# The end of an attention stage on one Trainium2 core: exponentials read straight from the banks, values by key tile, row sums spread by a product

## The chip, the cores and the metric

The kernel runs on one core of one Trainium2 chip. A core has five engines that run side by side and meet through semaphores: TensorE (PE in the profile, its weight loads PEld), VectorE (DVE), ScalarE (ACT), GpSimd (POOL) and SyncE (SP), which issues most DMAs. Matrix products go to eight banks of accumulator memory, from which DVE and ACT read. Everything else lies in the on-chip buffer (128 partitions) or in DRAM. A small q behind an engine's name (SPq, DVEq) means its sequencer, which loads registers, branches, waits and issues DMAs.

The metric is device time in microseconds of one execution; lower is better. Of several runs the median is taken.

## What is computed

From the reference: `x` is 2048 tokens of 448 features; 16 heads of 28 features share one key and one value projection; a token-mixing MLP runs beside the attention, and a sigmoid gate mixes the two.

```python
def _A_ref(x, wq, wk, wv, wo):
    B, S, D = x.shape
    H = 16
    Dh = D // H
    q = (lambda x, *d: x.transpose(*d))((x @ wq).reshape(B, S, H, Dh), 0, 2, 1, 3)
    k = x @ wk
    v = x @ wv
    scores = jnp.einsum("bhqd,bkd->bhqk", q, k) * (Dh ** -0.5)
    p = _softmax(scores, axis=-1)
    o = jnp.einsum("bhqk,bkd->bhqd", p, v)
    return (lambda x, *d: x.transpose(*d))(o, 0, 2, 1, 3).reshape(B, S, H * Dh) @ wo
...
x = A_x
g = _sigmoid((x * gate_w).sum(-1, keepdims=True))
a = _A_ref(x, A_wq, A_wk, A_wv, A_wo)
b = _B_ref(x, B_w1, B_w2, B_w3, B_w4)
return g * a + (1 - g) * b
```

## The kernel before

The MLP and the projections fill the first 410 us or so and are not touched. Attention is the last stage. It works through 16 units `u`: four blocks of 512 queries, and in each four groups of four heads. A unit has eight stretches `v` of two key tiles (128 keys each). All engines' instructions stand in the order in which the code writes them (`manual_schedule`); nothing is reordered later. The eight banks stand in a list: `take()` takes the first, whoever has read it last puts it back at the end (`banks.append`), and `bank(name)` does both at once.

A stretch (loop at line 886) does, in PE's order: scores of its two key tiles (`scores`, line 826, four heads in four banks for each), two half output products of an earlier unit (`wo_half`, line 807), and the value products of the stretch before (`values`, line 863). `exps` (line 845) turns the four score banks of a key tile into exponentials in the order `READ` = 0, 3, 1, 2. For heads 0, 1, 2, ACT does so straight from the bank (line 855). For head 3 (`DRAIN`), DVE copies the bank to the buffer (line 852), and at the end of the stretch `late_exps` (line 858) exponentiates the two copies in one pass of 1024 columns.

`values` multiplies, for each half of the 512 queries, both key tiles of all four heads with `vext`, whose first column is ones. Row 32j of the sum `o` therefore holds the sum of head j's exponentials; the 28 rows behind it hold the unnormalised output. Inside a unit DVE adds the banks into `o` (line 876). For all units but the last, the sums leave by a DMA that lays them out 128 x 16 (`sums_begin`, line 765), are checked against a limit and inverted (`recip`, line 770), go through DRAM and come back spread over 32 rows each (line 778); `norm` (line 781) multiplies. `wo_job` (line 787) multiplies 128 tokens with the output weights and adds the result, times the gate, to `ot`; in the last group of a block `ot` is sent out.

The last unit has no later work to hide behind. From line 915 on, its values are computed without adding, four additions of 128 queries follow (line 963), and PE transposes `o` by token tiles (line 968), so that the sums stand along the tokens: DVE then inverts 8 numbers per partition for two tiles (line 931) and multiplies (line 935); PE transposes back (line 940), ACT copies (line 941), and four `wo_job`s follow with `end` (line 946) as the last step: DVE adds for token tiles 0, 2, 3, ACT and POOL for tile 1, and SP (ACT for tile 1) issues the output's DMA. `keep_warm` puts small products into PE's waits.

The check of all sums ends in one number: `worst` per partition (line 982), transposed (line 989), reduced and turned to an integer flag (lines 992, 993). Every engine loads the flag (line 996) and branches over a slower fallback for the whole attention (line 999), which these inputs do not need. Behind it SP waits for all DMAs, and the engines meet at a barrier (line 1071 in the trace).

Of the kernel before, what the change touches and what calls it, by code (L numbers as in the profile page):

```python
# [9 lines left out]
F32 = mybir.dt.float32  # L10
F32R = mybir.dt.float32r
AF = mybir.ActivationFunctionType
ALU = mybir.AluOpType
# [29 lines left out]
def gated_mix_kernel(  # L43
# [686 lines left out]
    with tc.tile_pool(name="s3", bufs=1, reuse_waits="tile") as s3, \  # L730
# [7 lines left out]
        def take():  # L738
            return banks.pop(0)
# [15 lines left out]

        on_of = {}

        good = s3.tile([P, 8, 4], F32, name="good")
        nc.gpsimd.memset(good, 1.0)

        def check(sums, c):
            g = good[:, c:c + sums.shape[1]]
            nc.vector.scalar_tensor_tensor(g, sums, LIMIT, g, op0=ALU.is_le, op1=ALU.min)

        def sums_begin(u, o):
            rt = s3.tile([P, 16], F32, tag="rt", bufs=2, name=f"rt_{u}")
# [2 lines left out]

        def recip(u, o, rt, checked=True):  # L770
            if checked:
                check(rt.rearrange("p (a b) -> p a b", b=4), 0)
            rr = s3.tile([P, 16], F32, tag="rr", bufs=2, name=f"rr_{u}")
            nc.vector.reciprocal(rr, rt)
            rd = dram.tile([4, 512], F32, tag="rd", bufs=2, name=f"rd_{u}")
            nc.sync.dma_start(rd.rearrange("j (a b) -> (j a) b", b=16), rr)
# [7 lines left out]

        ot_of = {}

        def wo_job(u, t, end=None, cols=slice(0, D)):
            b, g = divmod(u, NG)
            n = 4 * b + t
            ps = take()  # L790
            for j in range(4):
                tok = slice(t * P + 32 * j, t * P + 32 * j + 32)
                nc.tensor.matmul(ps[32 * j:32 * j + 32, cols], on_of[u][:, tok], wof[:, g, cols],  # L793
                                 start=True, stop=True, tile_position=(0, 32 * j))
# [3 lines left out]
            if end:  # L798
                end(t, n, ps[:, 0:D], before)
            else:  # L800
                nc.vector.scalar_tensor_tensor(ot_of[n][:, cols], ps[:, cols], gg[:, n:n + 1], before,
                                               op0=ALU.mult, op1=ALU.add)
                if g == NG - 1 and cols.stop == D:
                    nc.sync.dma_start(out[0, n * P:(n + 1) * P, :], ot_of[n])
            banks.append(ps)

        def wo_half(u, i):
            t, h = divmod(i, 2)
            wo_job(u, t, None, slice(224 * h, 224 * h + 224))

        weigh_x1(NT - 4, NT)

# [29 lines left out]
            free.append(t)  # L842
            return t

        def exps(u, kt, bs):
            ps = p_of[u, kt] = {}
            for j in READ:
                if j == DRAIN:
                    if kt % 2 == 0:
                        pd_of[u, kt // 2] = turn_of(pd_free)  # L850
                    ps[j] = pd_of[u, kt // 2][:, kt % 2, :]
                    nc.vector.tensor_copy(ps[j], bs[j])  # L852
                else:
                    ps[j] = turn_of(p_free)
                    behind[kt % 2] = nc.scalar.activation(ps[j], bs[j], AF.Exp, scale=SCALE)  # L855
                banks.append(bs[j])

        def late_exps(u, v):
            pd = pd_of.pop((u, v))
            ins = nc.scalar.activation(pd, pd, AF.Exp, scale=SCALE)  # L860
            tc.add_manual_dep(ins.ins, behind[0].ins.name, SYNC, reason="one wait of ACT for its own writes per stretch")

        def values(u, v, add=True):
            if v == 0:
                o_of[u] = s3.tile([P, 512], F32, tag="o", bufs=2, name=f"o_{u}")
            pvs = []
            for q in (slice(0, 256), slice(256, 512)):
                pv = take()
                for kt in (2 * v, 2 * v + 1):
                    for j in range(4):  # L870
                        nc.tensor.matmul(pv[32 * j:32 * j + 32, q], vext[:, kt, :], p_of[u, kt][j][:, q],  # L871
                                         start=(kt % 2 == 0), stop=(kt % 2 == 1), tile_position=(0, 32 * j))
                if v == 0:
                    nc.vector.tensor_copy(o_of[u][:, q], pv[:, q])
                elif add:
                    nc.vector.tensor_add(o_of[u][:, q], o_of[u][:, q], pv[:, q])  # L876
                pvs.append(pv)
                if add:
                    banks.append(pv)
            return pvs  # L880

        READ = (0, 3, 1, 2)
        DRAIN = 3
        WO_AT = (4, 5, 6, 7)

        for k in range(NU * NV):
# [26 lines left out]
        assert not sums and not norms  # L913

        u = NU - 1
        pvs = values(u, NV - 1, False)
        o = o_of[u]
        on_of[u] = s3.tile([P, 512], F32, tag="on", bufs=2, name=f"on_{u}")
        toks = [slice(t * P, (t + 1) * P) for t in range(4)]
        tp = [bank(f"ot_{i}").rearrange("p (t n) -> p t n", t=4) for i in range(2)]  # L920
        tq = [bank(f"oq_{t}") for t in range(4)]
        spare = tq[3]
        tq = [ps[:, 0:P] for ps in tq]
        rr = s3.tile([P, 2, 2, 4], F32, name="rr4")
        on4 = s3.tile([P, 4, P], F32, name="on4")

        def sums_of(i):
            return tp[i][:, 0:2, 0:128:32]

        def tail_sums(i):  # L930
            nc.vector.reciprocal(rr[:, i], sums_of(i))

        def tail_on(t):
            i, k = divmod(t, 2)
            nc.vector.tensor_tensor(on4[:, t].rearrange("p (j d) -> p j d", j=4),
                                    tp[i][:, k].rearrange("p (j d) -> p j d", j=4),
                                    rr[:, i, k].unsqueeze(2).broadcast_to([P, 4, 32]), ALU.mult)

        def tail_back(t):
            nc.tensor.transpose(tq[t], on4[:, t], ident)  # L940
            nc.scalar.copy(on_of[u][:, toks[t]], tq[t])

        y = s3.tile([P, D], F32, name="y")
        outs = []

        def end(t, n, ps, before):
            if t == 1:
                nc.scalar.activation(y, ps, AF.Copy, scale=gg[:, n:n + 1])
                nc.gpsimd.tensor_tensor(ot_of[n], y, before, ALU.add)
            else:  # L950
                nc.vector.scalar_tensor_tensor(ot_of[n], ps, gg[:, n:n + 1], before, op0=ALU.mult, op1=ALU.add)
            queue = nc.scalar if t == 1 else nc.sync
            queue.dma_start(out[0, n * P:(n + 1) * P, :], ot_of[n])

        def tail_wo(t):
            wo_job(u, t, end)

        def keep_warm(n):
            for _ in range(n):
                nc.tensor.matmul(spare[:, 0:256], warm[:, 0:P], warm, start=True, stop=True)  # L960

        for t in range(4):
            nc.vector.tensor_add(o[:, toks[t]], o[:, toks[t]], pvs[t // 2][:, toks[t]])
        with tc.block():
            tc.mark_branch_hint_location("redo", "LikelyTaken", [mybir.EngineType.PE])
            keep_warm(5)
            for t in range(4):
                nc.tensor.transpose(tp[t // 2][:, t % 2], o[:, toks[t]], ident)
        keep_warm(3)
        tail_sums(0)  # L970
        tail_on(0)
        tail_on(1)
        tail_back(0)
        tail_back(1)
        keep_warm(2)
        tail_sums(1)
        tail_on(2)
        tail_on(3)
        for i in range(2):
            check(sums_of(i), 4 + 2 * i)  # L980
        worst = s3.tile([P, 1], F32, name="worst")
        nc.vector.tensor_reduce(worst, good, axis=AX.XY, op=ALU.min)
        tail_back(2)
        keep_warm(2)
        tail_wo(0)
        tail_back(3)
        tail_wo(1)
        tw = bank("worst_t")[0:1, 0:P]
        nc.tensor.transpose(tw, worst, ident)
        least = s3.tile([1, 1], F32, name="least")  # L990
        redo = s3.tile([1, 1], mybir.dt.int32, name="redo")
        nc.vector.tensor_reduce(least, tw, axis=AX.X, op=ALU.min)
        nc.vector.tensor_scalar(redo, least, -1.0, 1.0, op0=ALU.mult, op1=ALU.add)
        tail_wo(2)
        tail_wo(3)
        again = nc.values_load(redo, min_val=0, max_val=1)


# [76 lines left out]
```

## Time and profile before

| | us |
|---|---|
| median of 3 runs | 927.33 |
| lowest, highest | 925.99, 928.0 |
| the profiled execution | 926.66 |
| its span, from first to last instruction | 924.7 |
| granted TensorE clock in it, mean | 0.999 |

All durations are from the one profiled execution, whose span is 2.0 us shorter than its time. Times are counted from the start of the span. In a row of the timeline stand start, length, engine, line, operation, output<-inputs, shape and count; in brackets the engine's idle time before it and what ended it. A count over one merges neighbours; a float matrix product is recorded as two passes, so four heads make eight records.

The attention stage has 128 stretches. Between 910 and 914 us, in the last unit's own end, the engines were busy as follows (us of each):

| us from the start | PE | DVE | ACT | POOL |
|---|---|---|---|---|
| 910 to 912 | 2.00 | 1.07 | 0.00 | 0.00 |
| 912 to 914 | 1.85 | 1.53 | 0.72 | 0.00 |

### The profile page before, as it was taken

How to read it: one execution, taken by the hardware profiler on the slowest of the kernel's cores; microseconds unless marked ns; L12 is line 12 of the kernel's file. 1: busy time of each engine (PE TensorE's matmuls, PEld its weight loads, DVE VectorE, ACT ScalarE, POOL GpSimd, SP SyncE). 2: the span in 40 equal slices, each digit the busy share in tenths (PEclk: the TensorE clock that was granted, in tenths of full speed). 3: DMA queues.
4: the chain of work that ended last, by engine and by line, in shares of the span. 5: the costliest groups of instructions: out<-in, count | busy, mean ns of one | idle time of the engine just before them, and what ended most of it. 6: DMA issues, size and time to landing. Idle time of an engine off the chain costs nothing.

```text
span 924.7 us, 23960 instructions
## 1 busy us (share of the span) xinstructions
PE 911.7 (99%) x10051; PEld 647.5 (70%) x10051; DVE 542.2 (59%) x1081; ACT 634.5 (69%) x1134; POOL 104.2 (11%) x135
## 2 busy tenths in 40 slices
PE   9999999999999999999999999999999999999996
PEld 6788888888888888875566666666655656666663
DVE  4665263631435736446666666666666666666664
ACT  5542434432231232259999999999999999999993
POOL 2233200212000440031000000000000000000000
PEclk9999999999999999999999999999999999999999
DMA  9801534130122042110000001001011100110001
GB/s 303 300 27 26 169 128 129 22 84 21 33 65 60 19 104 61 38 54 23 25 23 6 26 14 53 26 26 26 8 41 46 26 4 24 35 45 3 14 14 44
DMA packets 40691, 50.72 MB, mean 55 GB/s; under 512 B 8752, under 2 KB 26880, under 8 KB 40576
## 3 DMA queue, kind: packets, MB, share of 16 engines
q1 hardware_dynamic: 37552, 43.65, 16.4%
q10 hardware_dynamic: 3024, 5.47, 1.6%
q8 instruction: 80, 1.31, 0.6%
q14 instruction: 35, 0.29, 0.1%
HBM read 37.04 MB, written 11.93 MB: 53 GB/s over the span
## 4 chain that ended last, share of the span: by engine, by line
PE 93%; ACT 3%; DMA 2%; DVE 1%; issue 0%; SPq 0%; DVEq 0%; ACTq 0%
PE bank L871 23%; PE bank L831 21%; PE bank L793 7%; PE acc L655 5%; PE acc L654 5%; PE acc L656 5%; PE g L132 4%; PE g L131 4%; PE g L133 4%; ACT p L855 2%; DMA xkv<-in_xT_dram 2%; PE hs L437 1%; PE hs L436 1%; PE hs L438 1%; PE g L135 1%; PE g L134 1%
## 5 line engine op out<-in xcount | busy, mean ns | idle before, releaser
L855 ACT ACTIVATE p<-bank 128x512 f32<-128x512 f32 x768 | 391.0, 626 | 5.8 <-PE bank L831 5.8
L871 PE MATMUL bank<-p,vext 128*32 128x256 f32 x3072 | 243.9, 379 | 2.1 <-ACT p L855 2.1
L871 PE MATMUL bank<-pd,vext 128*32 128x256 f32 x1024 | 242.2, 379 | 0.3 <-ACT pd L860 0.3
L852 DVE COPY pd<-bank 128x512 f32<-128x512 f32 x256 | 176.6, 691 | 53.2 <-PE bank L831 52.3
L871 PEld LDWEIGHTS bank<-p,vext 128*32 128x32 f32 x3072 | 125.1, 110 | 85.8 <-ACT p L855 5.1
L644 ACT ACTIVATE gh<-g 128x512 fp32r<-128x512 f32 x55 | 32.8, 597 | 189.5 <-PE g L135 189.5
L876 DVE TENSOR_TENSOR o<-o,bank 128x256 f32<-128x256 f32 x222 | 93.5, 421 | 91.3 <-ACT p L855 51.0
L860 ACT ACTIVATE pd<-pd 128x1024 f32<-128x1024 f32 x128 | 143.0, 1117 | 0.0
L831 PE MATMUL bank<-qh,kH 30*128 30x512 f32 x1024 | 119.6, 443 | 0.0
L871 PEld LDWEIGHTS bank<-pd,vext 128*32 128x32 f32 x1024 | 111.6, 110 | 1.3 <-ACT pd L860 0.7
L646 DVE TENSOR_TENSOR gl<-gf,gh 128x512 fp32r<-128x512 f32 x55 | 37.9, 690 | 125.5 <-ACT gf L645 125.4
L831 PE MATMUL bank<-qh,kL 28*128 28x512 f32 x1024 | 106.2, 394 | 0.0
L831 PE MATMUL bank<-ql,kH 28*128 28x512 f32 x1024 | 105.7, 389 | 0.0
L831 PEld LDWEIGHTS bank<-qh,kH 30*128 30x128 f32 x1024 | 60.9, 182 | 58.4 <-ACT p L855 47.0
L655 PE MATMUL acc<-w4l,gh 128*128 128x448 f32 x220 | 80.4, 366 | 0.0
L654 PE MATMUL acc<-w4h,gh 128*128 128x448 f32 x220 | 80.3, 365 | 0.0
L656 PE MATMUL acc<-w4h,gl 128*128 128x448 f32 x220 | 80.1, 364 | 0.0
L793 PE MATMUL bank<-wof,on 128*32 128x224 f32 (+1 forms) x992 | 73.1, 370 | 0.3 <-ACT p L855 0.3
L132 PE MATMUL g<-al,w3h 128*128 128x512 f32 x168 | 65.8, 392 | 0.0
L131 PE MATMUL g<-ah,w3h 128*128 128x512 f32 x168 | 65.6, 390 | 0.0
L133 PE MATMUL g<-ah,w3l 128*128 128x512 f32 x168 | 65.5, 390 | 0.0
L831 PEld LDWEIGHTS bank<-ql,kH 28*128 28x128 f32 x1024 | 52.6, 185 | 8.3
(196 smaller groups left out, 1164.8 us busy)
## 6 DMA issues: line engine op xcount, KB each, us to landing
qd<-qf ACTq DMA_DIRECT2D x16, 256.0 KB
qm<-qd SPq DMA_DIRECT2D x16, 256.0 KB
qr<-qd SPq DMA_DIRECT2D x16, 256.0 KB
rb<-rd SPq DMA_DIRECT2D x15, 256.0 KB
x<-in_x_dram SPq DMA_DIRECT2D x4, 896.0 KB
xd<-xt SPq DMA_DIRECT2D x16, 224.0 KB
w34raw<-in_w_dram SPq DMA_DIRECT2D x7, 512.0 KB
out_dram<-ot SPq DMA_DIRECT2D x15, 224.0 KB
```

Of the source, the lines that this page charges most:

```text
L131: nc.tensor.matmul(ps, wh[:, c, :], ah[:, c, :], start=(c == 0), stop=False)
L132: nc.tensor.matmul(ps, wh[:, c, :], al[:, c, :], start=False, stop=False)
L133: nc.tensor.matmul(ps, wl[:, c, :], ah[:, c, :], start=False, stop=False)
L654: nc.tensor.matmul(ps, gh[:, tok], w4h[i][:, k, :], start=(f == 0), stop=False)
L655: nc.tensor.matmul(ps, gh[:, tok], w4l[i][:, k, :], start=False, stop=False)
L656: nc.tensor.matmul(ps, gl[:, tok], w4h[i][:, k, :], start=False, stop=(f == stop))
L793: nc.tensor.matmul(ps[32 * j:32 * j + 32, cols], on_of[u][:, tok], wof[:, g, cols], start=True, stop=True, tile_position=(0, 32 * j))
L831: nc.tensor.matmul(bs[j], w, a, start=(i == 0), stop=(i == 2), tile_position=(32 * j, 0))
L852: nc.vector.tensor_copy(ps[j], bs[j])
L855: behind[kt % 2] = nc.scalar.activation(ps[j], bs[j], AF.Exp, scale=SCALE)
L860: ins = nc.scalar.activation(pd, pd, AF.Exp, scale=SCALE)
L871: nc.tensor.matmul(pv[32 * j:32 * j + 32, q], vext[:, kt, :], p_of[u, kt][j][:, q], start=(kt % 2 == 0), stop=(kt % 2 == 1), tile_position ...
```

## The change

It rewrites the end of the last unit. In the very last stretch no bank is drained by DVE: all eight exponentials are read by ACT from the banks, and there is no late pass. Its value products go by key tile, first both halves of tile 14, then both of tile 15, and two additions of 256 queries follow. The sums are no longer brought to the tokens by transposing: a matrix `spread` of ones in four 32 x 32 patterns (row 32j to columns 32j to 32j+31) is multiplied with `o`, so that each row of a bank holds its head's sum. DVE inverts that bank over all 512 queries (in pieces of 128, 128, 256) and multiplies. The check of the last unit's sums takes the DMA path that the other units use. Tiles 0, 1, 2 are finished by `wo_job` with DVE's addition, tile 3 in two halves of 224 columns; SP and ACT issue the outputs in turn. The flag is computed after all of that. Of twelve warming products two are left.

```diff
-        good = s3.tile([P, 8, 4], F32, name="good")
+        good = s3.tile([P, 4, 4], F32, name="good")
         nc.gpsimd.memset(good, 1.0)
+        spread = s3.tile([P, P], F32, name="spread")
+        nc.gpsimd.memset(spread, 0.0)
+        for j in range(4):
+            nc.gpsimd.memset(spread[32 * j:32 * j + 1, 32 * j:32 * j + 32], 1.0)
...
-        def wo_job(u, t, end=None, cols=slice(0, D)):
+        def wo_job(u, t, cols=slice(0, D), send=None):
...
+            nc.vector.scalar_tensor_tensor(ot_of[n][:, cols], ps[:, cols], gg[:, n:n + 1], before,
+                                           op0=ALU.mult, op1=ALU.add)
+            if send:
+                send(n, cols)
+            elif g == NG - 1 and cols.stop == D:
+                nc.sync.dma_start(out[0, n * P:(n + 1) * P, :], ot_of[n])
...
-        def exps(u, kt, bs):
+        def exps(u, kt, bs, drain=True):
             ps = p_of[u, kt] = {}
             for j in READ:
-                if j == DRAIN:
+                if drain and j == DRAIN:
...
+        def value(u, kt, i, pv):
+            q = HALVES[i]
+            for j in range(4):
+                nc.tensor.matmul(pv[32 * j:32 * j + 32, q], vext[:, kt, :], p_of[u, kt][j][:, q],
+                                 start=(kt % 2 == 0), stop=(kt % 2 == 1), tile_position=(0, 32 * j))
...
+            last = k == NU * NV - 1
             for kt in (2 * v, 2 * v + 1):
-                exps(u, kt, scores(u, kt))
-            late_exps(u, v)
+                exps(u, kt, scores(u, kt), not last)
+            if not last:
+                late_exps(u, v)
...
+        pvs = [take(), take()]
+        for kt in (NT - 2, NT - 1):
+            for i in range(2):
+                value(u, kt, i, pvs[i])
+        for i, q in enumerate(HALVES):
+            nc.vector.tensor_add(o[:, q], o[:, q], pvs[i][:, q])
+            banks.append(pvs[i])
...
+        def spread_sums(i):
+            nc.tensor.matmul(bc[i][:, HALVES[i]], spread, o[:, HALVES[i]], start=True, stop=True)
...
+        def divide(a, b):
+            nc.vector.reciprocal(rb[:, a:b], bc[a // 256][:, a:b])
+            nc.vector.tensor_mul(on_of[u][:, a:b], o[:, a:b], rb[:, a:b])
+
+        def store(n, cols):
+            queue = nc.scalar if n % 2 else nc.sync
+            queue.dma_start(out[0, n * P:(n + 1) * P, cols], ot_of[n][:, cols])
+
+        keep_warm(2)
         with tc.block():
             tc.mark_branch_hint_location("redo", "LikelyTaken", [mybir.EngineType.PE])
...
+            spread_sums(0)
+        _, _, rt = sums_begin(u, o)
+        spread_sums(1)
+        divide(0, 128)
+        divide(128, 256)
+        divide(256, 512)
+        for t in range(3):
+            wo_job(u, t, send=store)
+            if t == 1:
+                check(rt)
+                worst = s3.tile([P, 1], F32, name="worst")
+                nc.vector.tensor_reduce(worst, good, axis=AX.XY, op=ALU.min)
+        for h in range(2):
+            wo_job(u, 3, slice(224 * h, 224 * h + 224), store)
+        tw = sent[0:1, 0:P]
         nc.tensor.transpose(tw, worst, ident)
         least = s3.tile([1, 1], F32, name="least")
         redo = s3.tile([1, 1], mybir.dt.int32, name="redo")
         nc.vector.tensor_reduce(least, tw, axis=AX.X, op=ALU.min)
         nc.vector.tensor_scalar(redo, least, -1.0, 1.0, op0=ALU.mult, op1=ALU.add)
-        tail_wo(2)
-        tail_wo(3)
         again = nc.values_load(redo, min_val=0, max_val=1)
```

More of the change, by code (lines that the diff above doesn't have):

```diff
@@ L756, in gated_mix_kernel, with check @@
         on_of = {}
[L758 removed]
+        good = s3.tile([P, 4, 4], F32, name="good")
         nc.gpsimd.memset(good, 1.0)
[L761 to L763 removed]
+        spread = s3.tile([P, P], F32, name="spread")
+        nc.gpsimd.memset(spread, 0.0)
+        for j in range(4):
+            nc.gpsimd.memset(spread[32 * j:32 * j + 1, 32 * j:32 * j + 32], 1.0)
+        def check(rt):
+            nc.vector.scalar_tensor_tensor(good, rt.rearrange("p (a b) -> p a b", b=4), LIMIT, good,
+                                           op0=ALU.is_le, op1=ALU.min)
         def sums_begin(u, o):
@@ L915, in gated_mix_kernel @@
         u = NU - 1
-        pvs = values(u, NV - 1, False)
         o = o_of[u]
-        on_of[u] = s3.tile([P, 512], F32, tag="on", bufs=2, name=f"on_{u}")
[L919 to L956, printed above, removed]
+        pvs = [take(), take()]
+        for kt in (NT - 2, NT - 1):
+            for i in range(2):
+                value(u, kt, i, pvs[i])
+        for i, q in enumerate(HALVES):
+            nc.vector.tensor_add(o[:, q], o[:, q], pvs[i][:, q])
+            banks.append(pvs[i])
+        on_of[u] = s3.tile([P, 512], F32, tag="on", bufs=2, name=f"on_{u}")
+        spare = bank("warm")
+        sent = bank("worst_t")
+        bc = [bank(f"spread_{i}") for i in range(2)]
         def keep_warm(n):
```

58 lines of the change are left out of this document (11 added, 47 removed).

## The prediction

> **What bounds the kernel now.** I read the page first: the span, the busy shares and the row of granted clocks.
>
> ```profile
> span 924.7 us, 23960 instructions
> ...
> PE 911.7 (99%) x10051; PEld 647.5 (70%) x10051; DVE 542.2 (59%) x1081; ACT 634.5 (69%) x1134; POOL 104.2 (11%) x135
> ...
> PEclk9999999999999999999999999999999999999999
> ```
>
> TensorE is busy for 99% of the span, but the change touches nothing before the last stretch of attention, so only the last 20 us count. There the second view, the chain of waits from 904 us on, says what each moment waited for (columns: start, length, what ran).
>
> ```profile
> 908.02 0.94 ACT pd L860
> ...
> 909.01 1.91 PE bank L871 x26
> 910.92 0.65 PE bank L960 x5
> ...
> 911.92 0.20 DVE rr L931
> ...
> 913.68 0.89 PE bank L793 x8
> ...
> 917.69 0.68 DVE ot L951
> ```
>
> It is a single thread with no cover: ACT's late exponential, the last value products, transpositions, reciprocals, output products at 913.7, and the last addition on DVE, which ends at 918.37. After that 6.3 us remain with no computation. Those are the third view, the rows of line 996 (each engine loads the redo flag) and line 999 (each branches on it; what follows the branch is the first instruction behind the skipped code). Columns: line, engine, operation, count; shortest/median/longest ns; first and last start.
>
> ```profile
> L996 PEldq TENSOR_LOAD <-redo x1: 487/487/487, 916.5 to 916.5; - x1
> ...
> L996 SPq TENSOR_LOAD <-redo x1: 763/763/763, 918.8 to 918.8; - x1
> ```
>
> ```profile
> L999 SPq EVENT_SEMAPHORE  x8: 17/17/17, 922.8 to 923.3; - x8
> ...
> L999 PEldq COMPARE_BRANCH  x1: 998/998/998, 917.1 to 917.1; - x1
> L999 POOLq EVENT_SEMAPHORE  x1: 17/17/17, 917.7 to 917.7; - x1
> ...
> L999 ACTq COMPARE_BRANCH  x1: 54/54/54, 918.7 to 918.7; - x1
> L999 SPq COMPARE_BRANCH  x1: 45/45/45, 919.9 to 919.9; - x1
> ...
> L999 ACTq EVENT_SEMAPHORE  x1: 17/17/17, 922.6 to 922.6; - x1
> ```
>
> SP is the last to arrive. It loads the flag at 918.8, right behind its last output DMA, branches at 919.9, runs its next instruction at 922.8, and the span ends at 924.7. So the end is SP's load plus 5.9 us. Today the flag is ready early (PE loads it at 916.5) and SP's last DMA, hence the last addition, sets that load. The measure for the change is therefore one number: when SP can load the flag, against 918.8.
>
> **The change, part by part.** All times below are on the clock of this execution.
>
> *Exponentials of the last stretch.* Two DVE copies and one 1024-wide ACT pass go; two 512-wide ACT passes come. ACT's rows:
>
> ```profile
> 904.98 3.04 ACT L855 ACTIVATE p<-bank 128x512 f32<-128x512 f32 x6 [0.30 <-PE bank L831]
> 907.85 1.10 ACT L860 ACTIVATE pd<-pd 128x1024 f32<-128x1024 f32 x1
> ```
>
> From the first to the late one are six steps in 2.87, so 0.48 each, and one lasts 3.04 - 5 x 0.48 = 0.64. The eighth would start at 904.98 + 7 x 0.48 = 908.33 and end at 908.97; the late pass ended at 908.95. No gain on ACT. A cost: the drained score bank was freed by DVE, in parallel, and is now ACT's second; the bank that the value products of the stretch before need is ACT's third instead of its second. It comes free at 904.98 + 2 x 0.48 + 0.64 = 906.57 or so, and PE needs it at 906.41 (next fence). With about 0.03 for the semaphore PE stands 0.19 there.
>
> *Values by key tile.* PE's rows of the value products:
>
> ```profile
> 906.41 0.39 PE L871 MATMUL bank<-p,vext 128*32 128x256 f32 x3
> ...
> 908.13 0.61 PE L871 MATMUL bank<-p,vext 128*32 128x256 f32 x6
> 909.01 0.40 PE L871 MATMUL bank<-pd,vext 128*32 128x256 f32 x1 [0.27 <-ACT pd L860]
> ```
>
> From 906.41 to 908.13 eight passes run, 0.215 each; four heads over half the queries of one key tile are two passes, 0.43. At 908.13 PE could start the last stretch and stands until 909.01, because each half begins with a head whose exponentials come last; all eight passes then follow. By key tile the four passes of tile 14 fill that hole: 908.13 + 0.19 = 908.32, to 909.18, past the last exponential at 908.97. Tile 15 takes 0.86, to 910.04. Before, these ended at 909.01 + 1.72 = 910.73. Gain 0.69; without the bank's wait 0.16 more, as then the last exponential holds PE (908.97 plus 0.05); if the hole stays, nothing.
>
> *Adding, spreading the sums.* DVE's rows of the old tail, and the shapes that price the new one (mean ns before the last bar's idle time):
>
> ```profile
> 910.96 0.49 DVE L963 TENSOR_TENSOR o<-o,bank 128x128 f32<-128x128 f32 x2 [0.32 <-PE bank L871]
> ...
> 912.14 0.49 DVE L935 TENSOR_TENSOR on<-bank,rr 128x128 f32<-128x128 f32 x2
> 912.55 0.20 DVE L931 RECIPROCAL rr<-bank 128x8 f32<-128x8 f32 x1
> ...
> 914.63 0.68 DVE L951 SCALAR_TENSOR_TENSOR ot<-bank,gg,ot 128x448 f32<-128x448 f32 x1 [1.00 <-PE bank L793]
> ```
>
> ```profile
> L876 DVE TENSOR_TENSOR o<-o,bank 128x256 f32<-128x256 f32 x222 | 93.5, 421 | 91.3 <-ACT p L855 51.0 <-PE bank L871 40.3
> L801 DVE SCALAR_TENSOR_TENSOR ot<-bank,gg,ot 128x224 f32<-128x224 f32 x88 | 38.6, 442 | 0.0
> ...
> L774 DVE RECIPROCAL rr<-rt 128x16 f32<-128x16 f32 x15 | 3.7, 246 | 0.0
> ...
> L951 DVE SCALAR_TENSOR_TENSOR ot<-bank,gg,ot 128x448 f32<-128x448 f32 x3 | 2.1, 684 | 1.5 <-PE bank L793 1.5
> ...
> L935 DVE TENSOR_TENSOR on<-bank,rr 128x128 f32<-128x128 f32 x4 | 1.0, 286 | 0.1
> ...
> L931 DVE RECIPROCAL rr<-bank 128x8 f32<-128x8 f32 x2 | 0.4, 204 | 0.5 <-PE bank L968 0.5
> L992 DVE TENSOR_REDUCE least<-bank 1x1 f32<-1x128 f32 x1 | 0.3, 279 | 0.7 <-PE bank L989 0.7
> ...
> L763 DVE SCALAR_TENSOR_TENSOR good<-bank,good 128x8 f32<-128x8 f32 x2 | 0.2, 156 | 0.0
> L982 DVE TENSOR_REDUCE worst<-good 128x1 f32<-128x32 f32 x1 | 0.2, 186 | 0.0
> ...
> L993 DVE TENSOR_SCALAR redo<-least 1x1 int32<-1x1 f32 x1 | 0.1, 141 | 0.0
> ```
>
> DVE began the last addition 0.23 after PE's last pass (910.96 against 910.73). So the two additions of 256 run at 909.84 to 910.26 and 910.27 to 910.69. The product of the ones matrix with the first half needs a 128x128 float weight load and two passes of 256 columns. The nearest row is such a load in the first stage; below it an output product of the old tail:
>
> ```profile
> 23.38 0.41 PEld L396 LDWEIGHTS wsum_ps<-wsum,ones 128*128 128x128 f32 x2
> ```
>
> ```profile
> 913.61 0.96 PE L793 MATMUL bank<-wof,on 128*32 128x448 f32 x8
> ```
>
> Half of 0.41 for the load (0.2), 0.215 to the second pass, 0.38 for that pass (the 256-column row above), 0.05 for the semaphore at each end: 910.26 + 0.05 + 0.2 + 0.215 + 0.38 + 0.09 (from PE's end to DVE's start) gives 911.19. The second product ends while DVE divides, and costs nothing.
>
> *The division, the largest term.* The old tail takes 16 reciprocals per row of the partitions, the new one 512, all on DVE and in order: 128, 128 and 256, each followed by its multiplication. No row has a wide reciprocal. The two that exist differ by 8 elements and 42 ns; of the two of 8, the one that follows work directly is 0.20 (912.55), as the one of 16 does with 0.246: 47 ns, 5.9 ns an element, and 0.15 fixed, which is also what the other narrow DVE rows leave. Bounds: below, 1.04 ns an element, as (421 - 286)/128 gives for a multiplication; above, 7.9 ns, if the fixed part were only the 141 ns of the smallest row (204 - 141 over 8). I take 5.9, nearest the rows that are reciprocals: 0.91 for 128, 1.66 for 256. Two independent DVE instructions overlap by 0.08 (0.49 for two of 0.286); a dependent one starts 0.03 later. First reciprocal 911.19 to 912.10, product to 912.42; second 912.34 to 913.25, product to 913.57; third 913.49 to 915.15, product to 915.60.
>
> [...]
>
> *Output products.* PE starts token tile 0 at about 912.47 and tile 1 at 913.62. Tiles 2 and 3 wait for the third division, 915.65; DVE started on a tile 1.02 after PE did (914.63 against the 913.61 above), so tile 2 is ready at 916.67. DVE is behind anyway: its four additions stand in its queue after all divisions. Tile 0 915.52, tile 1 916.12 to 916.80 (0.60 apart); the check 0.16, and the reduction that depends on it 0.19, to 917.10; tile 2 917.02 to 917.70; the halves of tile 3, 0.36 apart, to 918.42. Tile 1 was ACT's and POOL's before, and ended there at no cost to the path; now it costs DVE 0.60.
>
> *The flag.* Its last reduction and conversion stood between other additions; now they are DVE's last: 918.34 to 918.62 and 918.65 to 918.79. Every engine's load waits for it; behind SP's and ACT's loads only their branches are queued, and their last DMAs are issued ahead. SP loads at 918.83.
>
> *At nothing:* the new sums transfer. Its row and the one of what follows it in the loop:
>
> ```profile
> L767 SPq DMA_DIRECT2D rt<-o x15: 544/559/621, 444.0 to 880.1; - x15
> ```
>
> ```profile
> L776 SPq DMA_DIRECT2D rd<-rr x15: 319/321/329, 448.1 to 884.3; - x15
> ```
>
> Issue to used reciprocals is at most 4.2 us; issued at 910.7 it is needed at 916.7. If it took 2 us longer than that bound, the excess would go to DVE's path. It is also ahead of SP's output DMAs by 5 us. The five fills of the ones matrix fall at the stage's start on POOL, which is busy for 11% of the span (first fence). The dropped warming products cost nothing: PE now stands at most 1.2 us (tile 1 to tile 2), while the granted clock stayed at full to the last slices of the page.
>
> **Sum.** The values end 0.69 earlier (910.04 for 910.73). From there to the last addition it was 918.37 - 910.73 = 7.64 and becomes 918.42 - 910.04 = 8.38, 0.74 longer. SP's load follows 0.41 after that addition, for the flag, where it followed 0.43 after it, for a DMA. So 918.83 against 918.8: no change; the span stays 924.7. This execution took 926.66, 0.67 less than the median 927.33 of the runs; on the median's scale the forecast is 927.4. Its own range is 926.6 to 928.3: one ns an element more or less in the division (0.5), the bank's wait (0.2), and 0.3 across the branch.
>
> **Rivals.**
>
> A. *A wide reciprocal runs at an element a cycle,* the excess being start-up. The three divisions then take 512 x 4.9 ns = 2.5 us less, and PE and DVE stay close: 924.9. Against it: the excess over other DVE rows grows from 48 ns at 8 elements (204 - 156) to 82 at 16 (246 less 156 and 8 elements of 1.04). 0.10.
>
> B. *It runs at the rows' upper bound,* 7.9 ns: 512 x 2.0 = 1.0 more, 928.4. For it: two rows with so little between them bound it no closer. [...] Against it: the fixed part it needs is smaller than that of any DVE row of such width. 0.18.
>
> C. *Slower: the branch becomes the bound.* Now PE and POOL are past it by 918, and ACT branches 1.2 us ahead of SP. With the flag last, all five branch within 0.6 us. ACT's gap across the branch was 3.9 us, SP's 2.9. If the code behind it is brought in for one engine after another, ACT goes on at 919.4 + 3.9 = 923.3 and SP 0.2 later, 0.7 over my sum, and PE's 1.0 and POOL's 0.6 come into the same stretch: up to +2.3, 929.7. It decides once SP's gap exceeds 2.9. Against it: nothing shows that they share a path. 0.18.
>
> D. *The hole in PE stays,* that is, the values gain nothing (a bank or a semaphore that holds tile 14 until ACT is done): +0.7, 928.1. Against it: all four exponentials of tile 14 end by 907.1. 0.08.
>
> **How the numbers follow.** The forecast has 0.46. 0.2% is 1.85 us, what a measurement of this kernel can tell from no change: 925.5 and 929.2. Faster: A and 0.02 of the forecast, 0.12. Slower: two thirds of C, a quarter of B (with some of C's cost on top), 0.02 of the forecast: 0.19. The rest, 0.69, is within. The range 925.9 to 929.3 leaves out A and about half of C.
>
> **What would show it.** Right: eight exponentials ending near 908.97, the last values near 910.0, reciprocals of 0.9, 0.9 and 1.7 us, DVE without a gap from 911.2 to 918.8, SP's load at about 918.8 and 2.9 us across its branch. Wrong: reciprocals under 0.4 or over 1.1 for 128, a gap before the check (the sums are late), SP's gap well over 3 us, or outputs that land after SP asks for them.

## The result, and the profile after

| | before | after |
|---|---|---|
| median of 20 runs, us | 927.78 | 929.66 |
| lowest, highest | 925.42, 929.36 | 927.67, 930.46 |
| the profiled execution, us | 926.66 | 927.67 |
| its span, us | 924.7 | 925.9 |

The ratio of the two is 1.0019, with the interval 1.0012 to 1.0025: a small loss, 1.1 to 2.3 us by the interval, where no change was forecast, and 0.36 us outside the range. The forecast started from a median of 927.33 for the kernel before, 0.45 below the one here; but for that the number would lie inside the range, so what counts is the step between the two kernels. The page of the kernel after begins:

```profile
span 925.9 us, 23942 instructions
...
PE 910.5 (98%) x10045; PEld 645.6 (70%) x10045; DVE 544.6 (59%) x1078; ACT 633.8 (68%) x1130; POOL 103.2 (11%) x139
```

Most engines issue a few instructions less than before; POOL issues four more, 139 for 135. That will matter.

The two spans can't be set against each other directly. What the change touches begins with the first score product of the last stretch, and in the executions profiled here that product started anywhere from 903.31 to 906.75 us. So all times of the end are counted here from that product, the mark, and "the way" is the time from the mark to the end of the span (924.73 and 925.89 by the finer ends in the trace). In the timelines of PE (start, length) the mark stands in the first row. Before:

```profile
903.97 0.50 PE L831 MATMUL bank<-qh,kH 30*128 30x512 f32 x4
```

After, with the first value product of the stretch before, which waits for a bank, and the value products of the last stretch:

```profile
903.83 0.51 PE L834 MATMUL bank<-qh,kH 30*128 30x512 f32 x4
...
906.46 0.42 PE L869 MATMUL bank<-p,vext 128*32 128x256 f32 x3
...
908.21 1.91 PE L869 MATMUL bank<-p,vext 128*32 128x256 f32 x32
...
915.68 1.72 PE L797 MATMUL bank<-wof,on 128*32 128x448 f32 x24 [1.17 <-DVE on L947]
```

In the last row PE stands 1.17 for DVE's third product before the output products of tiles 2 and 3, 0.03 off the forecast wait of 1.2. The way was 924.73 - 903.97 = 20.76 before and is 925.89 - 903.83 = 22.06 after: 1.30 us more. ACT's row after shows all eight exponentials in one group, from bank to buffer:

```profile
904.83 4.03 ACT L858 ACTIVATE p<-bank 128x512 f32<-128x512 f32 x8 [0.29 <-PE bank L834]
```

They end 908.86 - 903.83 = 5.03 after the mark; the late pass before ended 4.98 after it. The 32 value passes now run as one group without a hole and end 910.12 - 903.83 = 6.29 after the mark, for 910.92 - 903.97 = 6.95: 0.66 gained, as forecast. DVE's timeline shows where it goes:

```profile
909.81 0.85 DVE L929 TENSOR_TENSOR o<-o,bank 128x256 f32<-128x256 f32 x2 [0.87 <-PE bank L869]
911.02 0.96 DVE L946 RECIPROCAL rb<-bank 128x128 f32<-128x128 f32 x1 [0.36 <-PE bank L941]
912.01 0.29 DVE L947 TENSOR_TENSOR on<-o,rb 128x128 f32<-128x128 f32 x1
912.22 0.95 DVE L946 RECIPROCAL rb<-bank 128x128 f32<-128x128 f32 x1
913.21 0.29 DVE L947 TENSOR_TENSOR on<-o,rb 128x128 f32<-128x128 f32 x1
913.41 1.75 DVE L946 RECIPROCAL rb<-bank 128x256 f32<-128x256 f32 x1
915.20 0.42 DVE L947 TENSOR_TENSOR on<-o,rb 128x256 f32<-128x256 f32 x1
915.54 1.27 DVE L802 SCALAR_TENSOR_TENSOR ot<-bank,gg,ot 128x448 f32<-128x448 f32 x2
916.73 0.16 DVE L766 SCALAR_TENSOR_TENSOR good<-rt,good 128x16 f32<-128x16 f32 x1
...
917.01 1.39 DVE L802 SCALAR_TENSOR_TENSOR ot<-bank,gg,ot 128x448 f32<-128x448 f32 x3
918.32 0.27 DVE L974 TENSOR_REDUCE least<-bank 1x1 f32<-1x128 f32 x1
918.62 0.14 DVE L975 TENSOR_SCALAR redo<-least 1x1 int32<-1x1 f32 x1
```

From 911.0 to the flag DVE has no gap in brackets: it alone sets the pace. The last addition ends at 918.40, 14.57 after the mark, for 918.37 - 903.97 = 14.40 before. Up to here the change costs 0.17. The rest lies behind it. The rows of the two lines with the load of the flag and the branch, after:

```profile
L976 SPq TENSOR_LOAD <-redo x1: 723/723/723, 918.8 to 918.8; - x1
```

```profile
L979 SPq EVENT_SEMAPHORE  x8: 17/17/17, 924.0 to 924.5; - x8
L979 POOLq COMPARE_BRANCH  x1: 45/45/45, 919.6 to 919.6; - x1
L979 ACTq COMPARE_BRANCH  x1: 54/54/54, 919.6 to 919.6; - x1
L979 DVEq COMPARE_BRANCH  x1: 72/72/72, 919.6 to 919.6; - x1
L979 PEldq COMPARE_BRANCH  x1: 430/430/430, 919.6 to 919.6; - x1
L979 SPq COMPARE_BRANCH  x1: 45/45/45, 919.9 to 919.9; - x1
L979 POOLq EVENT_SEMAPHORE  x1: 17/17/17, 920.1 to 920.1; - x1
...
L979 ACTq EVENT_SEMAPHORE  x1: 17/17/17, 923.8 to 923.8; - x1
```

SP loads at 918.8 and branches at 919.9, as before to the tenth, and goes on at 924.0 where it went on at 922.8. From the finer starts in the trace, this gap of SP across its branch is 4.05, for 2.86. Of 1.30 on the way 1.19 is here. No landing of an output holds SP: the eight semaphores follow each other at 0.07, and by the trace the last output landed at 920.3.

The last view is that of the DMA queues in the stretch around the branch, which counts the pieces of program code that are brought in (packets, MB, share). Before, from 919 to 922.7:

```profile
q8 instruction: 1, 0.02, 2.0%
q14 instruction: 3, 0.02, 1.9%
```

After, from 919.5 to 924:

```profile
q14 instruction: 4, 0.03, 2.7%
q8 instruction: 1, 0.02, 1.4%
```

Queue 14 brings four pieces where it brought three; a piece is 8 KB (in the trace each is recorded as 8192 bytes). The record doesn't name the engine that a piece is for. Pieces are counted below only around the branch: those that start between the first engine's branch and 2 us behind SP's. Three more follow further on, by the trace from 2.9 us behind SP's branch before and from 4.5 after.

The first theory was rival C's: that five engines branching at once makes each wait longer. The second was that another engine now calls for one more piece of code there.

### The profile page after: what moved, and what is told of

The parts are those of the page before. It is cut to its first block, busy times and chain, and to the rows that moved or that the text cites. A ratio compares the mean times of both kernels' runs of the same rounds, so it can differ in the third digit from the quotient of the medians.

```text
span 925.9 us, 23942 instructions
## 1 busy us (share of the span) xinstructions
PE 910.5 (98%) x10045; PEld 645.6 (70%) x10045; DVE 544.6 (59%) x1078; ACT 633.8 (68%) x1130; POOL 103.2 (11%) x139
## 4 chain that ended last, share of the span: by engine, by line
PE 95%; ACT 2%; DVE 1%; DMA 0%; issue 0%; ACTq 0%
PE bank L869 23%; PE bank L834 21%; PE bank L797 7%; PE acc L655 5%; PE acc L654 5%; PE acc L656 5%; PE g L132 4%; PE g L131 4%; PE g L133 4%; ACT p L858 2%; PE hs L437 1%; PE hs L436 1%; PE hs L438 1%; PE g L135 1%; PE g L134 1%; PE h L131 1%
```

## The experiments

All of them in one table, in the order in which they ran. The ratio is to the kernel before, run on the same chip; "last" is the end of the last addition behind the mark, "gap" SP's across its branch, "pieces" those of queue 14, counted as above. Early and late tell whether the flag is computed among or behind the output products.

| kernel | flag | ratio, 95% interval | way | last | gap | pieces |
|---|---|---|---|---|---|---|
| before | early | | 20.8 | 14.4 | 2.86 | 3 |
| after | late | 1.0019, 1.0012 to 1.0025 | 22.1 | 14.6 | 4.05 | 4 |
| a_again | late | 1.0011, 1.0002 to 1.0019 | 21.9 | 14.6 | 3.85 | 4 |
| b_flag_late | late | 0.9994, 0.9985 to 1.0003 | 20.5 | 14.1 | 2.90 | 3 |
| a_flag_early | early | 1.0007, 0.9997 to 1.0018 | 21.1 | 14.9 | 3.58 | 4 |
| b_values | early | 0.9985, 0.9976 to 0.9995 | 20.4 | 13.7 | 3.15 | 3 |
| b_pool4 | early | 1.0006, 0.9996 to 1.0015 | 21.1 | 14.4 | 3.02 | 4 |
| a_pool | late | 0.9998, 0.9990 to 1.0007 | 21.1 | 14.6 | 3.06 | 3 |
| b_values_late | late | 0.9991, 0.9982 to 1.0001 | 19.7 | 13.4 | 2.77 | 3 |
| a_whole | late | 1.0015, 1.0006 to 1.0024 | 21.5 | 14.5 | 3.78 | 4 |
| b_pool4_late | late | 1.0010, 1.0001 to 1.0018 | 21.4 | 14.1 | 3.79 | 4 |
| a_pool_early | early | 0.9998, 0.9989 to 1.0007 | 21.1 | 14.9 | 3.58 | 3 |
| a_pool2 | late | 1.0008, 0.9999 to 1.0017 | 21.5 | 14.6 | 3.54 | 3 |
| b_values_late2 | late | 0.9985, 0.9976 to 0.9994 | 19.9 | 13.4 | 2.99 | 3 |
| a_pool3 | late | 1.0017, 1.0008 to 1.0026 | 21.6 | 14.6 | 3.54 | 3 |
| b_pool4_late2 | late | 1.0011, 0.9999 to 1.0022 | 21.6 | 14.1 | 4.02 | 4 |
| b_flag_late2 | late | 0.9999, 0.9990 to 1.0008 | 20.5 | 14.0 | 2.96 | 3 |
| b_pool12_late | late | 1.0013, 1.0004 to 1.0021 | 21.5 | 14.1 | 3.87 | 4 |

**a_again: the kernel after once more,** unchanged.

> The changed kernel once more, for a second profile and for its time on the same chip as the next three. Theory (the flag last, so that all five engines branch at once and the code behind the branch reaches SP late): SP's gap from branch to next instruction again near 4.0 us where the kernel before shows 2.9; time 1.2 to 2.0 us over before. Rival (the 4.0 was this one profile's accident): a gap anywhere from 2.8 to 4 that does not go with the kernel.

The gap is 3.85 and the last addition 14.6 after the mark: the two findings repeat, in an execution that reached the mark 2.7 us later (906.53).

**b_flag_late: the kernel before with the flag behind all outputs,** and nothing else.

```diff
+        tail_wo(2)
+        tail_wo(3)
         tw = bank("worst_t")[0:1, 0:P]
...
-        tail_wo(2)
-        tail_wo(3)
```

> The kernel before with one edit: the flag's transposition, reduction and conversion are put behind the last output product. Theory: SP's load starts at most 0.1 us later than before (its DMA ends about when the flag is there), yet SP's gap across the branch grows from 2.9 to about 4.0, and the time by 1.1 to 1.9 us. Rival one (the outputs in halves on ACT's queue, or their smaller packets, delay the code): the gap stays at 2.9 and the time within 0.3 us of before. Rival two (an accident of one profile): the same, no change.

All five engines branch within half a microsecond of each other, yet the gap is 2.90. It was 2.96 in the repetition (b_flag_late2), whose rows show the branches as close together as after, with SP's last: ACT 920.1, POOL 920.2, SP 920.5, and SP's next instruction at 923.5.

```profile
L999 SPq EVENT_SEMAPHORE  x8: 17/17/17, 923.5 to 924.0; - x8
L999 ACTq COMPARE_BRANCH  x1: 54/54/54, 920.1 to 920.1; - x1
L999 POOLq COMPARE_BRANCH  x1: 45/45/45, 920.2 to 920.2; - x1
...
L999 POOLq EVENT_SEMAPHORE  x1: 17/17/17, 920.4 to 920.4; - x1
L999 SPq COMPARE_BRANCH  x1: 45/45/45, 920.5 to 920.5; - x1
```

In the old end branching together costs SP's gap nothing by itself (2.90 and 2.96 for the 2.86 before); the first theory falls. A side result: with the transposition of `worst` out from between the output products the last addition comes 0.3 earlier.

**a_flag_early: the kernel after with the flag ahead of the last three additions.**

```diff
+        check(rt)
...
             if t == 1:
-                check(rt)
-                worst = s3.tile([P, 1], F32, name="worst")
-                nc.vector.tensor_reduce(worst, good, axis=AX.XY, op=ALU.min)
+                flag()
```

> The changed kernel with one edit: check and worst stand behind the second division, transposition, reduction and conversion behind the third, so that the flag is known about 2 us before the last addition. DVE has the same work. Theory: PE and POOL branch early, SP loads right behind its last DMA, about 0.2 us earlier than in the changed kernel, and its gap falls to about 2.9; ACT, behind the last output DMA, may end the span instead; 0.8 to 1.6 us faster than the changed kernel. Rival (halves of the output on ACT's queue): the gap stays near 4 and only 0.2 us is gained.

The gap goes to 3.58, not to the expected 2.9: 0.27 to 0.47 less than in the two profiles of the kernel after; the flag's reduction and conversion, now in front of the last additions, delay these by 0.36 (14.93 for 14.57). The ratio, 1.0007, can't be told from that of a_again on the same chip.

**b_values: the first half of the change alone,** exponentials from the banks and values by key tile, ahead of the old end with its transpositions.

```diff
...
-        pvs = values(u, NV - 1, False)
+        pvs = [take(), take()]
+        for kt in (NT - 2, NT - 1):
+            for pv, q in zip(pvs, (slice(0, 256), slice(256, 512))):
...
```

> The kernel before with the first half of the change alone: the last stretch's exponentials all from the banks, its values by key tile; the old tail with transpositions, the old place of the flag. Theory: the values end 0.7 to 0.8 us earlier and all behind them moves with them: 0.7 us faster than before, SP's gap as before. Rival (the gain is taken back, as code behind the branch arrives at a time of its own): the last addition 0.7 us earlier, the span unchanged.

The last addition ends 13.7 after the mark, 0.68 earlier than before, and the kernel is faster than both: 0.9985. In this profile 0.38 of the 0.68 reach the end of the span, since the gap is 3.15; so the rival, that the branch takes the gain back, is true in part. PE's row shows the 32 passes without a hole, as in the kernel after:

```profile
909.94 1.91 PE L921 MATMUL bank<-p,vext 128*32 128x256 f32 x32
```

**b_pool4: the kernel before with four small fills more on POOL,** as many instructions as the change adds there (five fills come, the addition of tile 1 goes). The tile they fill is not read.

```diff
+        more = s3.tile([P, 16], F32, name="more")
+        for j in range(4):
+            nc.gpsimd.memset(more[:, 4 * j:4 * j + 4], 1.0)
```

> The kernel before with four more POOL fills of 4 columns at the start of attention, so that POOL's stream is as long as in the changed kernel (205 instructions ahead of its branch in place of 201); nothing else. Theory (the four instructions make POOL bring in one more piece of code at the end, and the pieces share a path): a fourth 8 KB piece near the branch, SP's gap 3.6 to 4.1 us in place of 2.9, the way from the last stretch's first scores to the end 21.6 to 22.1 us in place of 20.8. Rival (the output in halves on ACT's queue): gap 2.9, way 20.8.

The fourth piece is there, but the gap is 3.02, so the expectation missed. With the flag early POOL branches 3.1 us ahead of SP (919.4 and 922.5), and a piece comes at 920.5, two microseconds ahead of SP's branch: it is out of the way. Only POOL and PE had branched by then (DVE did at 920.7), and PE's program is as before, so this piece is put down to POOL's branch. The 0.4 us on the way come from SP's load of the flag, which lies 0.4 later behind the mark; why isn't known.

**b_pool4_late, b_pool4_late2, b_pool12_late: the same four fills with the flag late, twice, and twelve fills.**

```diff
-        for j in range(4):
+        for j in range(12):
```

> The kernel before with both edits that alone changed SP's gap little (2.90 and 3.02 us): the flag computed last, and four more POOL fills. Theory (POOL's extra piece of code costs the end when POOL branches together with the others): POOL's gap rises from 0.18 to about 0.46, four pieces of 8 KB near the branch, SP's gap 3.7 to 4.1, the way from the last stretch's first scores to the end 21.3 to 21.7 us where the late flag alone had 20.51; some 1 us slower than with the late flag alone. Rival (something in the changed kernel's tail, its outputs or its products, sets the gap): 2.9 to 3.1, way 20.5 to 20.7.

> The kernel before with late flag and four more POOL fills, a second profile. Theory: four pieces, gap 3.6 to 4.1 again (3.79 the first time). Rival (variation): about 3.

> As with the late flag and four more POOL fills, but with twelve more. Theory (a piece of code is brought in or not): the same four pieces and the same gap as with four, 3.6 to 4.1. Rival (each POOL instruction costs at the end, or fills as such): the gap grows further, to 5 or more.

The rows of b_pool4_late2 against those of b_flag_late2 above, of which it differs by the four fills:

```profile
L1002 SPq EVENT_SEMAPHORE  x8: 17/17/17, 926.5 to 927.0; - x8
...
L1002 POOLq COMPARE_BRANCH  x1: 45/45/45, 922.0 to 922.0; - x1
...
L1002 SPq COMPARE_BRANCH  x1: 45/45/45, 922.4 to 922.4; - x1
L1002 POOLq EVENT_SEMAPHORE  x1: 17/17/17, 922.5 to 922.5; - x1
```

SP stands 4.0 for 3.0, and POOL goes on 0.46 after its branch in place of 0.18. Queue 14 in the stretch of that branch, first in b_flag_late2, then in b_pool4_late2, then with twelve fills:

```profile
q14 instruction: 3, 0.02, 1.9%
```

```profile
q14 instruction: 4, 0.03, 2.5%
```

```profile
q14 instruction: 4, 0.03, 2.4%
```

With the old end and the flag late, three pieces go with gaps of 2.77, 2.90, 2.96 and 2.99, four pieces with 3.79, 3.87 and 4.02. Twelve fills cost what four do (3.87 for 3.79 and 4.02, with four pieces each time): between none, four and twelve it is a step, one more piece, and not a price for each instruction. In the time, 0.9994 and 0.9999 stand against 1.0010, 1.0011 and 1.0013, with intervals that overlap; on the one chip on which three of them ran together (b_flag_late2 927.43, b_pool4_late2 928.51, b_pool12_late 928.54) it is 1.1 us in the medians.

**a_pool, a_pool2, a_pool3: the kernel after with the fills of `spread` on DVE,** three times.

```diff
-        nc.gpsimd.memset(spread, 0.0)
+        nc.vector.memset(spread, 0.0)
...
-            nc.gpsimd.memset(spread[32 * j:32 * j + 1, 32 * j:32 * j + 32], 1.0)
+            nc.vector.memset(spread[32 * j:32 * j + 1, 32 * j:32 * j + 32], 1.0)
```

> The changed kernel with the five fills of the ones matrix on DVE in place of POOL, so that POOL has 200 instructions ahead of its branch. Theory (POOL's extra piece of code): three pieces near the branch, SP's gap 2.8 to 3.2 us in place of 3.9 to 4.05, way from the last stretch's first scores to the end 20.9 to 21.1 us in place of 21.9 to 22.1; about 1 us faster than the changed kernel. Rival (halves of the output): no change.

> The changed kernel with the fills on DVE, once more, for a second profile. Theory (POOL's piece of code): POOL's gap 0.18, three pieces of 8 KB near the branch, SP's gap 2.9 to 3.2 us, way from the last stretch's first scores to the end 20.9 to 21.2, time within 0.1% of before. Rival (the 3.06 was one execution's luck, the gap varies from 2.9 to 4 whatever the kernel): a gap of 3.6 or more.

> The changed kernel with the fills on DVE, a third profile: the first two showed SP's gap at 3.06 and 3.54 us. Theory (a fourth piece of code costs about 0.8 us): three pieces, gap under 3.6, POOL's gap 0.18. Rival (the gap varies by itself from 2.8 to 4): as likely over 3.6 as under.

The piece is gone each time, and POOL's gap is 0.18, as in b_flag_late. SP's gap falls to 3.06, 3.54 and 3.54, from 4.05, 3.85 and 3.78 with four pieces; the 2.9 to 3.2 expected of a_pool2 was missed. (DVE's program grows by the five fills, from 1560 to 1565 instructions ahead of its branch, as many as in the kernel before.) The rows of a_pool3, at one of the longer gaps:

```profile
L979 SPq EVENT_SEMAPHORE  x8: 17/17/17, 923.6 to 924.2; - x8
...
L979 POOLq EVENT_SEMAPHORE  x1: 17/17/17, 920.0 to 920.0; - x1
L979 SPq COMPARE_BRANCH  x1: 45/45/45, 920.1 to 920.1; - x1
```

```profile
q14 instruction: 3, 0.02, 2.3%
```

So some 0.5 us of the 1.19 go with the piece in the new end (the mean of three gaps is 3.38 for 3.89), where the old end shows 1.0 for it; one kernel's gap alone varies by 0.48 here. In the time the ratios 0.9998, 1.0008 and 1.0017 overlap with those of the kernel after, 1.0019, 1.0011, and of a_whole, 1.0015: a gain of moving the fills is likely, but it isn't settled.

**a_whole: tile 3 in one piece on SP's queue,** in place of two halves on ACT's.

```diff
-            queue = nc.scalar if n % 2 else nc.sync
+            queue = nc.scalar if n % 4 == 1 else nc.sync
...
-        for h in range(2):
-            wo_job(u, 3, slice(224 * h, 224 * h + 224), store)
+        wo_job(u, 3, send=store)
```

> The changed kernel with token tile 3 as one output product, one addition and one DMA on SP, as in the kernel before, in place of two halves on ACT's queue. Theory (POOL's extra piece of code sets SP's gap): gap stays 3.8 to 4.1 us, the way from the last stretch's first scores to the end 21.7 to 22.1. Rival (the halves on ACT's queue delay the code): gap 2.9, way about 21.

Gap 3.78, four pieces, ratio 1.0015: the halves on ACT's queue are not the cause.

**a_pool_early: the edits of a_pool and a_flag_early together,** fills on DVE and the flag early.

> The changed kernel with the fills on DVE and the flag early: both repairs together. Theory: without POOL's piece of code SP's gap is 2.8 to 3.1 us (3.58 with the early flag alone), the way from the last stretch's first scores to the end 20.4 to 20.8 (21.09 with the early flag alone, 20.76 in the kernel before): no slower than before. Rival (the early flag only moves the wait to ACT, which branches last): ACT's next instruction ends the span, way 21 or more.

A miss: three pieces, and the gap is 3.58 all the same, as in a_flag_early with four. It doesn't break the step found in the old end, but it shows that something else can lengthen the gap. The trace has a candidate, the landing of the outputs. In all five profiles with the flag early the last part of an output lands 2.6 to 3.3 us behind SP's branch, and SP goes on 0.1 to 0.5 us after it (in the kernel before it lands at 922.67, 2.72 behind the branch, and SP goes on 0.14 later). In the thirteen with the flag late all outputs have landed by 0.9 us behind the branch, and SP goes on 1.9 to 3.6 us after that (in the kernel after they have landed at 920.34, 0.43 behind it, and SP goes on 3.62 later). In a_flag_early and a_pool_early, where ACT issues the last half 0.5 us ahead of SP's branch and itself branches 0.5 behind it, the last landings are the latest (3.13 and 3.32, for 2.56 to 2.78 in the three with the old end) and the gaps the longest of the five. Whether SP waits for these landings, or for code on a way that it might share with the outputs, wasn't tried; either way a gap with the flag early isn't a measure of the pieces alone.

**b_values_late, b_values_late2: the edits of b_values and b_flag_late together,** the first half of the change with the flag late, twice.

> The kernel before with the first half of the change (exponentials all from the banks, values by key tile) and the flag computed last; the old transpositions stay. Both alone shortened the way from the last stretch's first scores to the end, by 0.37 and 0.25 us. Theory: the last addition ends 13.4 us after those scores (14.4 before), the flag is there at 13.8, SP's gap 2.9: way 19.8 to 20.0, 0.8 to 1.0 us faster than before. Rival (the branch's pieces of code take it back): gap over 3.4, way 20.4 or more.

> The version with the shortest way so far (values by key tile, old transpositions, late flag), once more. If the way of 19.69 us holds, the time is 1 us under the kernel before; if the first time, 0.9991 of before, is nearer, half of it.

The last addition ends 13.4 after the mark, as expected, and the gap stays at 2.77 and 2.99. The ratios are 0.9991 and 0.9985, the way is 19.7 and 19.9, the shortest of all. Beside a_pool (same pieces, flag late in both, last addition at 14.6) this prices the second half of the change, the sums spread over rows: 1.2 us later at the last addition, since DVE's three reciprocals and their products take from 911.0 to 915.6 where the old end inverts 16 numbers a partition.

## Why the prediction was wrong

**Right, exponentials and bank wait.** ACT gains nothing (5.03 for 4.98 after the mark). PE's wait for the third bank: the value products of the stretch before begin 906.46 - 903.83 = 2.63 after the mark, for 906.41 - 903.97 = 2.44 before: 0.19, as forecast.

**Right, values by key tile.** 0.66 for 0.69; the hole was filled, so rival D is out. PE did not stand through all of the hole, as the prediction has it: it ran the first products of three heads (908.13, x6) and was idle for 0.27. But the fourth head's passes set the end, so the hole was worth what the sum took. b_values shows it as a gain in the time too.

**Right in kind, a little short: the division.** The reciprocals took 0.96, 0.95 and 1.75 where 0.91, 0.91 and 1.66 stood; the sum was short by 0.18. From 128 to 256 elements the time grows by 1.75 - 0.95 = 0.80, 6.25 ns an element. Two rows of 8 and 16 elements had given 5.9. Rival A (1.04) and rival B (7.9) are both out.

**Right, DVE's order and SP's load.** Tile 1 on DVE, the sums back in time for the check (DVE reached the check at 916.73 without a gap; by the trace they had landed at 912.5, 1.8 behind their issue; the bound of 4.2 was too low for one of the 15 earlier units, which took 4.5), the flag last: SP loads at 918.8, the forecast 918.83. On the mark's clock it is 0.14 later than before, which that number hid, as this execution reached the mark 0.14 earlier.

**Wrong, "the end is SP's load plus 5.9 us", with "0.3 across the branch" in its own range.** Load to end is 925.9 - 918.8 = 7.1. The 1.2 more lie in SP's gap across the branch, 4.05 for 2.86, which the prediction had named as a sign of being wrong. The old value was carried over as if it were fixed for SP, but even in the old end with the flag late it is 2.77 to 2.99 with three pieces on queue 14 and 3.79 to 4.02 with four.

**Wrong, a term put at nothing: "The five fills of the ones matrix fall at the stage's start on POOL".** When they run they cost nothing: they fill 403.9 to 404.7 on POOL, which behind them still stands 0.48 for DVE. With them POOL's program is four instructions longer (205 ahead of its branch for 201), and four pieces of code come around the branch for three. With the flag late the fourth falls into the same stretch as the other three, behind which SP, DVE and ACT go on (in the kernel after the pieces move from 920.56 to 921.37, DVE and ACT go on at 923.8, SP at 924.0). b_flag_late against b_pool4_late, each done twice, and b_pool4, done once, show both conditions in the old end: late alone 2.9 and 3.0, fills alone 3.0, late and fills 3.8 and 4.0. In the new end, the change itself, this is some 0.5 of the 1.19. That the fourth piece is POOL's is inferred, from its coming and going with POOL's fills, from its time in b_pool4, and with the flag late from POOL's gap (0.46 for 0.18). With the flag early POOL's gap is no sign of it: 0.59 in the kernel before, with three pieces. POOL itself does not wait for it: in the kernel after POOL goes on at 920.1, and no piece starts before 920.5.

**Rival C** had the place and the sign, though it allowed up to 2.3 us where 1.19 was found; that its 929.7 is so near the median of 929.66 is chance. Its mechanism, five branches at once with the code for one engine after another, isn't what was found: in the old end five branches at once leave SP's gap at 2.90 and 2.96, and with a piece more it is 3.79 to 4.02.

**Open.** Of the new end's 1.19, some 0.5 stays when the fourth piece is gone (3.06, 3.54 and 3.54 for the old end's 2.77 to 2.99). It isn't tile 3's halves, and in the old end the common branch costs SP's gap nothing (2.90 and 2.96 for 2.86); whether it is where the branches and their targets lie in the code wasn't tried. For the 3.58 of a_pool_early the late landings of the outputs are a candidate, not tested.

## What to carry to other kernels

Put nothing at zero because its engine is idle: here four small fills made POOL's program longer, and in the old end with the flag late, at the branch that all engines take, one more piece of code came with them and SP's gap was a microsecond longer (3.89 on average for 2.90). Compare ends from a common mark, because what lies ahead of it can drift by more than the effect (here from 903.31 to 906.75, for an effect of 1.30). And split a change that gains nothing: here the first half gains (0.9985 with the flag early, 0.9991 and 0.9985 with it late, 926.39 against 928.02 in b_values_late2), and the second gives it back; the version to keep is the exponentials from the banks and values by key tile, with the old way of the sums.

## What the runs showed of the hardware

In the kernel after a reciprocal on DVE from a bank took 6.25 ns an element ((1.75 - 0.95) us over 128) and 0.15 us fixed (0.95 less 128 x 6.25 ns), six times the 1.05 ns an element of the multiplication behind it (425 less 291 ns, over 128, line 947).

From the branch over the fallback to the next instruction it took SP 2.86 us, DVE 3.87, ACT 3.89, POOL 0.59 and PE 1.06 in the kernel before, and 4.05, 4.17, 4.19, 0.46 and 0.49 in the kernel after. Around it queue 14 brings three pieces of 8 KB before and four after, for which engines isn't recorded, and queue 8 one of 16 KB each time. By the trace these pieces of 8 KB took 0.31 to 0.40 us each to move before and 0.42 to 0.55 after, while with the fourth SP's gap is longer by 1.0 in the old end with the flag late (3.89 on average for 2.90 with three). What happens between the end of the last of them and SP's next instruction, 1.5 us before and 2.6 after, is not in the profile.
